# One ones column instead of two, hardware queues only, the last store on the last semaphore, one group's weight sums moved: four small edits to a transformer block bound by TensorE

## The chip, the cores and the metric

The kernel runs on one core of a Trainium2 chip. The metric is the device time of one execution, in microseconds (us); a time below is the median of several executions, with the lowest and highest beside it. A profile shows one execution from inside; its span is about 1.8 us shorter than the device time of the same execution (1271.0 against 1272.77 us for the kernel before), so spans are compared with spans and device times with device times. Engines are named as the profile names them: PE is TensorE's matmul side, PEld its weight load, DVE is VectorE, ACT is ScalarE, POOL is GpSimd, SP is SyncE, which issues most DMAs.

## The reference

A transformer block in bf16: modulation vectors from a small vector `c`, attention of 32 query heads over the last 512 keys of 4 key-value heads, and a gated MLP.

```python
mod = (silu(c) @ w_mod).reshape(1, 6, 1, 1024)        # sa, ca, ga, sb, cb, gb
h = layernorm(x) * (1 + ca) + sa                      # x: 2048 x 1024
q = h @ wq                                            # wq: 1024 x 4096, 32 heads of 128
p = softmax(q k^T * 128**-0.5)                        # k, v: the last 512 of 2048 positions
x = x + ga * ((p v) @ wo)                             # wo: 4096 x 1024
h = layernorm(x) * (1 + cb) + sb
x = x + gb * ((silu(h @ w_gate) * (h @ w_up)) @ w_down)   # 1024 x 3584, 3584 x 1024
```

## The kernel before

The sequence of 2048 rows is worked in four chunks of 512. One chunk and one head make a unit, so there are 128 units. In each unit PE makes scores (`s_ps`), ACT exponentiates them to `pT`, and PE multiplies them with V (`o_ps`): four row tiles times four key tiles, 2048 small matmuls in all. In between, PE makes the queries of a later unit (`q_ps`) and the output projection of an earlier chunk (`a_ps`). After the attention come the MLP's products (`gu_ps`, `d_ps`). The parts that the change touches follow; `[...]` marks cuts.

The divisor of the softmax is made by PE: columns of ones stand beside V, so a column of the product is the row's sum. There are two of them, and only the first is read. Three row tiles share a PSUM bank.

```python
    VN = Dh + 2                                        # Dh = 128
    v_sb = const.tile([P, Hkv, WT, Dh + 32], BF16, name="v_sb")
    [...]
    nc.gpsimd.memset(v_sb[:, :, :, Dh:VN], 1.0)
    [...]
    SLOTS = 3
    def close_bank():
        [...]
        nc.vector.reciprocal(out=rl[:, 0:n], in_=ps[:, 0:n, Dh])
        [...]   # oq = ps[.., 0:Dh] * rl, on DVE
    def emit_o(g):
        [...]
        for t in range(QT):
            if o_slot["n"] == 0:
                o_slot["ps"] = mm("o_ps", (P, SLOTS, VN))
            s_ = o_slot["n"]
            for j in range(WT):
                nc.tensor.matmul(o_slot["ps"][:, s_, :], lhsT=pT[g][:, j, t * P:(t + 1) * P],
                                 rhs=v_sb[:, kv, j, 0:VN], start=(j == 0), stop=(j == WT - 1))
            [...]
            if o_slot["n"] == SLOTS or (t == QT - 1 and h % HQ == HQ - 1):
                close_bank()
```

The first weights for the queries come in pieces of 512 KB; the first of them is loaded in two halves. The loads of V come later, one for each key-value head.

```python
    def load_wq8(i):
        t = blkB("wq8", [P, 2, 8 * P])
        for j in range(2 * i, 2 * i + 2) if i == 0 else ():
            load(t[:, j % 2, :], wq_v[:, j, 0:8 * P])
        if i > 0:
            load(t, wq_v[:, 2 * i:2 * i + 2, 0:8 * P])
    [...]
    def load_v(kv):
        load(v_sb[:, kv, :, 0:Dh], v_v[:, kv])
```

The exponentials are taken without subtracting a maximum. While it runs, the kernel therefore adds up squares of the weights (`bound_wq`, four DVE passes for each group of four heads) and, if a bound is passed, computes everything again by a slower general path behind `tc.If`. With these inputs that path never runs. `at` puts a task into the work of a unit; with `hg` 3 the four passes fall into chunk 1.

```python
    def bound_wq(hg, i, j):
        w = wq_tiles[(1 + hg % (NTC - 1), hg, i)][:, 2 * j:2 * j + 2, :]    # NTC = 4 chunks
        [...]   # one pass of DVE over 128 x 1024, accumulated into sq
    [...]
    at((1 + hg % (NTC - 1)) * H + 4 * hg - LEAD + 2 * i + j, bound_wq, hg, i, j)
    [...]
    def emit_down(cc, dh, t, widths=(512,)):           # the last tile: widths (256, 128, 128)
        [...]
        nc.scalar.dma_start(out=out2d[row:row + P, dsl], in_=o)     # the stores, on ACT's queue
    [...]
        with tc.If(over > 0):
            general_path(tc, *args)                    # three of its DMAs are issued by GpSimd
```

Of the kernel before, what the change touches and what calls it, by code (L numbers as in the profile page):

```python
# [23 lines left out]
def general_path(  # L24
# [16 lines left out]
    nc = tc.nc  # L41
    P = 128
# [3 lines left out]
    H = HD // Dh  # L46
# [121 lines left out]
    with tc.tile_pool(name="atsb", bufs=3) as ap_, tc.tile_pool(  # L168
# [7 lines left out]
        ln_psum["pool"], ln_psum["tag"] = aps, "mm"  # L176
        cT = const.tile([P, DT], BF16, name="cT")
        with nc.allow_non_contiguous_dma(reason="tiny c load"):
            nc.gpsimd.dma_start(out=cT, in_=c_v)
        sig_c = const.tile([P, DT], FP32, name="sig_c")  # L180
        nc.scalar.activation(out=sig_c, in_=cT, func=ACT.Sigmoid)
        siluc = const.tile([P, DT], BF16, name="siluc")
# [12 lines left out]
        with tc.tile_pool(name="p1small", bufs=3) as p1s:  # L195
# [16 lines left out]
            def mod_group(g, late=False):  # L212
                if late:
                    if H * P >= DT * GW:
                        wmf = ap_.tile([P, H, P], BF16, name="wm_l", tag="wo_t", bufs=2)
                        wm = wmf.rearrange("p h q -> p (h q)")[:, 0:DT * GW].rearrange(
                            "p (dt g) -> p dt g", dt=DT)
                    else:
                        wm = ap_.tile([P, DT, GW], BF16, name="wm_l2", tag="wm_late", bufs=2)
                    eng = nc.gpsimd  # L220
                else:
                    wm = op_.tile([P, DT, GW], BF16, name="wm", tag="oT")
                    eng = nc.sync
                with nc.allow_non_contiguous_dma(reason="w_mod column group"):
                    eng.dma_start(out=wm, in_=wm_v[:, :, g * GW:(g + 1) * GW])
                row_ps = aps_s.tile([1, GW], FP32, name="row_ps", tag="s_ps")
                for dt in range(DT):
                    nc.tensor.matmul(row_ps, lhsT=siluc[:, dt:dt + 1], rhs=wm[:, dt, :],
                                     start=(dt == 0), stop=(dt == DT - 1))
                row_sb = ap_.tile([1, GW], FP32, name="row_sb", tag="wq_h", bufs=5)  # L230
                if late:
                    nc.vector.tensor_copy(out=row_sb, in_=row_ps)
                else:
                    nc.scalar.copy(out=row_sb, in_=row_ps)
                for jj in range(JJ):
                    j = (g * GW) // P + jj
                    nc.tensor.matmul(modT_ps[:, j:j + 1], lhsT=row_sb[0:1, jj * P:(jj + 1) * P],
                                     rhs=one11[0:1, 0:1], start=True, stop=True)
                if g == n_first - 1:
                    nc.vector.tensor_copy(out=modT[:, 0:2 * DT], in_=modT_ps[:, 0:2 * DT])  # L240
                    nc.vector.tensor_scalar(out=onepc1, in0=modT[:, DT:2 * DT], scalar1=1.0,
                                            scalar2=None, op0=ALU.add)
                if g == NG - 1:
                    nc.vector.tensor_copy(out=modT[:, 2 * DT:NMOD], in_=modT_ps[:, 2 * DT:NMOD])
                    nc.vector.tensor_scalar(out=onepc2, in0=modT[:, 4 * DT:5 * DT], scalar1=1.0,
                                            scalar2=None, op0=ALU.add)
# [283 lines left out]
    with tc.tile_pool(name="ffw", bufs=2) as fw, tc.tile_pool(  # L530
        name="ffgu", bufs=2) as fgu, tc.tile_pool(
        name="ffsb", bufs=2) as fsb, tc.tile_pool(
        name="ffps", bufs=2, space=bass.MemoryType.PSUM) as fps, tc.tile_pool(
        name="ffps2", bufs=1, space=bass.MemoryType.PSUM) as fps2:
        ln_psum["pool"], ln_psum["tag"] = fps2, "o_ps"
        for f in leftovers:
            f()
        for tci in range(NTC):
            tsl = slice(tci * TCW, (tci + 1) * TCW)
            hsrc = h2T[tci]  # L540
            guT = fgu.tile([P, FT, TCW], BF16, name="guT", tag="guT")
            for fg in range(NFG):
                wg = fw.tile([P, DT, FG * P], BF16, name="wg", tag="wg")
                wu = fw.tile([P, DT, FG * P], BF16, name="wu", tag="wu")
                with nc.allow_non_contiguous_dma(reason="ffn weight slices"):
                    nc.sync.dma_start(out=wg, in_=wg_v[:, :, fg * FG * P:(fg + 1) * FG * P])
                    nc.sync.dma_start(out=wu, in_=wu_v[:, :, fg * FG * P:(fg + 1) * FG * P])
                for fi in range(FG):
                    f = fg * FG + fi
                    g_ps = fps.tile([P, TCW], FP32, name="g_ps", tag="g_ps")  # L550
                    for dt in range(DT):
                        nc.tensor.matmul(g_ps, lhsT=wg[:, dt, fi * P:(fi + 1) * P],
                                         rhs=hsrc[:, dt, :], start=(dt == 0), stop=(dt == DT - 1))
                    u_ps = fps.tile([P, TCW], FP32, name="u_ps", tag="u_ps")
                    for dt in range(DT):
                        nc.tensor.matmul(u_ps, lhsT=wu[:, dt, fi * P:(fi + 1) * P],
                                         rhs=hsrc[:, dt, :], start=(dt == 0), stop=(dt == DT - 1))
                    sig = fsb.tile([P, TCW], BF16, name="sig", tag="sig")
                    nc.scalar.activation(out=sig, in_=g_ps, func=ACT.Sigmoid)
                    g1 = fsb.tile([P, TCW], BF16, name="g1", tag="g1")  # L560
                    nc.vector.tensor_tensor(out=g1, in0=g_ps, in1=sig, op=ALU.mult)
                    nc.vector.tensor_tensor(out=guT[:, f, :], in0=g1, in1=u_ps, op=ALU.mult)
            xf = fsb.tile([P, DT, TCW], BF16, name="xf", tag="xf", bufs=1)
            for dc in range(DT):
                wd = fw.tile([P, FT, P], BF16, name="wd", tag="wd")
                with nc.allow_non_contiguous_dma(reason="w_down column slice"):
                    nc.sync.dma_start(out=wd, in_=wd_v[:, :, dc * P:(dc + 1) * P])
                d_ps = fps.tile([P, TCW], FP32, name="d_ps", tag="d_ps")
                for f in range(FT):
                    nc.tensor.matmul(d_ps, lhsT=wd[:, f, :], rhs=guT[:, f, :],  # L570
                                     start=(f == 0), stop=(f == FT - 1))
                nc.vector.scalar_tensor_tensor(out=xf[:, dc, :], in0=d_ps,
                                               scalar=gb[:, dc:dc + 1], in1=xT[:, dc, tsl],
                                               op0=ALU.mult, op1=ALU.add)
            for qt in range(QT):
                o_ps = fps2.tile([P, DT, P], BF16, name="o_ps", tag="o_ps")
                for dt in range(DT):
                    nc.tensor.transpose(o_ps[:, dt, :], xf[:, dt, qt * P:(qt + 1) * P], ident)
                o_sb = fsb.tile([P, D], BF16, name="o_sb", tag="o_sb")
                if qt % 2 == 0:  # L580
                    nc.vector.tensor_copy(out=o_sb, in_=o_ps.rearrange("p a b -> p (a b)"))
                else:
                    nc.scalar.copy(out=o_sb, in_=o_ps.rearrange("p a b -> p (a b)"))
                row0 = tci * TCW + qt * P
                nc.gpsimd.dma_start(out=out2d[row0:row0 + P, :], in_=o_sb)


@with_exitstack
def fast_path(ctx, tc, flag, A_x, A_k_cache, A_v_cache, A_wq, A_wo, B_x, B_w_gate, B_w_up,
# [119 lines left out]

    def load_wq8(i):  # L710
        t = blkB("wq8", [P, 2, 8 * P])
        for j in range(2 * i, 2 * i + 2) if i == 0 else ():
            load(t[:, j % 2, :], wq_v[:, j, 0:8 * P])
        if i > 0:
            load(t, wq_v[:, 2 * i:2 * i + 2, 0:8 * P])
        wq8.append(t)

    for tt in range(QT):
# [6 lines left out]
    h10 = hpool.tile([P, DT, TCW], BF16, name="hT", tag="hT")  # L725
    load_wm(0, 1)
    kT = blkB("kT", [P, Hkv, W])
    VN = Dh + 2
    v_sb = const.tile([P, Hkv, WT, Dh + 32], BF16, name="v_sb")

    def load_kT(kv):
        pin(nc.sync.dma_start_transpose(
            out=kT[:, kv, :], in_=A_k_cache[0, kv, k0:k0 + W, :]), "dma")

    def load_v(kv):
        load(v_sb[:, kv, :, 0:Dh], v_v[:, kv])

    load_v(0)
    load_wq(0, 2, (0,))
# [2 lines left out]
    for kv in range(1, Hkv):  # L742
        load_kT(kv)
    for kv in range(1, Hkv):
        load_v(kv)

    ones_bf = const.tile([P, P], BF16, name="ones_bf")
    nc.vector.memset(ones_bf, 1.0)
# [88 lines left out]
    def at(k, f, *a):  # L837
        tasks.setdefault(k, []).append((f, a))
# [286 lines left out]
    sq = const.tile([P, NSQ], FP32, name="sq")  # L1125
    gd = const.tile([P, 4], FP32, name="gd")

    def bound_wq(hg, i, j):
        w = wq_tiles[(1 + hg % (NTC - 1), hg, i)][:, 2 * j:2 * j + 2, :]
        junk = wk.tile([P, 2, 512], BF16, name="junk", tag="junk", bufs=1)  # L1130
        col = (hg * 2 + i) * 2 + j
        pin(nc.vector.scalar_tensor_tensor(out=junk, in0=w, scalar=1.0, in1=w, op0=ALU.mult,  # L1132
# [174 lines left out]
    for hg in range(H // 4):  # L1307
        for i in range(2):
            for j in range(2):
                at((1 + hg % (NTC - 1)) * H + 4 * hg - LEAD + 2 * i + j, bound_wq, hg, i, j)  # L1310
    at(NU - H + 2, load_k)
    for kv in range(Hkv):
        at(NU - H + 20 + 2 * kv, bound_k, kv)
# [165 lines left out]
```

## Time and profile before

| | kernel before |
|---|---|
| device time, median of 3 (lowest to highest) | 1272.97 us (1272.22 to 1273.32) |
| span of the profiled execution | 1271.0 us |
| PE busy | 1263.9 us, 99% |
| first `o_ps` matmul starts | 34.03 us |
| first MLP matmul (`gu_ps`) starts | 664.96 us |
| last matmul starts | 1265.92 us |

These are the head of the profile's page, its line of busy times, and the first line of the chain of work that ended last:

```profile
span 1271.0 us, 18169 instructions
PE 1263.9 (99%) x7589; PEld 641.3 (50%) x7589; DVE 608.6 (48%) x1332; ACT 335.6 (26%) x440; POOL 4.2 (0%) x15
PE 97%; DVE 1%; ACT 0%; DMA 0%; POOL 0%; issue 0%; SPq 0%
```

PE is busy nearly always and the chain is almost all PE. Such a kernel is made faster in three ways only: fewer PE columns, fewer gaps of PE, or a shorter head and tail. The 48% of DVE means nothing by itself.

The next view is that of the groups of instructions by shape. Its columns are line, engine, operation, output and inputs, shape, count; then the busy time, the mean duration of one in ns, and the idle time of the engine before them. The second group is the last narrow pieces of the down product.

```profile
L1241 PE MATMUL o_ps<-v_sb,pT 128*128 128x130 bf16 x2048 | 137.0, 220 | 0.1
L1375 PE MATMUL d_ps<-wd,guT 128*128 128x128 bf16 x56 | 3.3, 219 | 0.0
```

The 220 ns are the time of one matmul from its start to its end as the profile models it; matmuls overlap, so what counts is the time from start to start. In the trace that is 56.7 ns for the 130-column `o_ps` matmuls, 55.8 ns for the 128-column `d_ps` pieces and 215.8 ns for 512 columns.

There is one gap of PE in the long middle. The view of windows shows it (columns: start and end in us, then for PE, PEld, DVE, ACT and POOL the busy us and number of instructions, then granted clock, DMA share and GB/s), then come the line of the waits between 200 and 232 us, two lines of PE's timeline and two of DVE's (start us, duration us, engine, line, what):

```profile
215.00:220.00 5.00, 5.00 (x37) 2.77 (x35) 5.00 (x10) 1.94 (x2) 0.00 (x0) 1.00 0.47 115
220.00:225.00 5.00, 5.00 (x24) 2.16 (x22) 5.00 (x13) 2.83 (x5) 0.00 (x0) 1.00 1.01 300
225.00:230.00 5.00, 4.86 (x41) 2.97 (x41) 5.00 (x12) 1.54 (x2) 0.00 (x0) 1.00 0.41 86
545.00:550.00 5.00, 5.00 (x37) 2.76 (x36) 3.63 (x9) 1.72 (x3) 0.00 (x0) 1.00 0.75 239
```

```profile
PEld L1241 <- DVE oq L1228: 0.3, 1, 0.3
```

```profile
223.97 1.03 PE L1209 MATMUL s_ps<-qT,kT 128*128 128x512 bf16 x4
225.14 1.12 PE L1241 MATMUL o_ps<-v_sb,pT 128*128 128x130 bf16 x17
```

```profile
220.80 1.22 DVE L1132 SCALAR_TENSOR_TENSOR junk<-wq 128x1024 bf16<-128x1024 bf16 x1
224.47 0.61 DVE L1228 TENSOR_TENSOR oq<-o_ps,rl 128x128 bf16<-128x128 f32 x2
```

DVE is busy for 15 of 15 us, so it divides an earlier bank of `o_ps` (the `oq` at 224.47 us) late. PE needs that bank back and stands for 0.30 us: four `s_ps` matmuls from 223.97 us would take 0.86 us, but the next one starts only at 225.14. One of the passes over the weights stands in DVE's queue shortly before (220.80 us, 1.22 us).

Three start times cut the execution into pieces: the first `o_ps`, the first `gu_ps` and the last matmul. Here are the first two in the timeline:

```profile
34.03 1.07 PE L1241 MATMUL o_ps<-v_sb,pT 128*128 128x130 bf16 x16
664.96 1.89 PE L1355 MATMUL gu_ps<-hT,wg 128*128 128x512 bf16 x8
```

### The profile page before, as it was taken

How to read it: one execution, taken by the hardware profiler on the slowest of the kernel's cores; microseconds unless marked ns; L12 is line 12 of the kernel's file. 1: busy time of each engine (PE TensorE's matmuls, PEld its weight loads, DVE VectorE, ACT ScalarE, POOL GpSimd, SP SyncE). 2: the span in 40 equal slices, each digit the busy share in tenths (PEclk: the TensorE clock that was granted, in tenths of full speed). 3: DMA queues.
4: the chain of work that ended last, by engine and by line, in shares of the span. 5: the costliest groups of instructions: out<-in, count | busy, mean ns of one | idle time of the engine just before them, and what ended most of it. 6: DMA issues, size and time to landing. Idle time of an engine off the chain costs nothing.

```text
span 1271.0 us, 18169 instructions
## 1 busy us (share of the span) xinstructions
PE 1263.9 (99%) x7589; PEld 641.3 (50%) x7589; DVE 608.6 (48%) x1332; ACT 335.6 (26%) x440; POOL 4.2 (0%) x15
## 2 busy tenths in 40 slices
PE   9999999999999999999999999999999999999998
PEld 4555555555555555555554444444444444444444
DVE  5666658885678664567564631321222112221122
ACT  3543334343333433334341111011100111011100
POOL 1000000000000000000000000000000000000000
PEclk9999999999999999999999999999999999999999
DMA  9997756768456555455585479326633565425702
GB/s 286 211 240 172 186 141 159 182 160 222 122 137 174 150 137 153 113 154 112 121 205 144 130 232 248 95 96 204 220 112 106 169 213 181 158 91 170 244 20 67
DMA packets 306860, 204.46 MB, mean 161 GB/s; under 512 B 145617, under 2 KB 303313, under 8 KB 306770
## 3 DMA queue, kind: packets, MB, share of 16 engines
q1 hardware_dynamic: 301858, 199.03, 57.7%
q10 hardware_dynamic: 4912, 4.20, 1.0%
q8 instruction: 61, 1.00, 0.3%
q14 instruction: 29, 0.24, 0.1%
HBM read 165.94 MB, written 4.21 MB: 134 GB/s over the span
## 4 chain that ended last, share of the span: by engine, by line
PE 97%; DVE 1%; ACT 0%; DMA 0%; POOL 0%; issue 0%; SPq 0%
PE gu_ps L1355 30%; PE a_ps L1273 17%; PE q_ps L1198 16%; PE d_ps L1375 15%; PE o_ps L1241 9%; PE s_ps L1209 8%; PE q_ps L1044 1%; DVE junk L1132 0%; DMA x<-in_A_x_dram 0%; DVE st L847 0%; DVE junk L818 0%; DVE oq L1228 0%; DVE qT L948 0%; DVE f L1286 0%; PE one_ps L1062 0%; DVE f L1285 0%
## 5 line engine op out<-in xcount | busy, mean ns | idle before, releaser
L1211 ACT ACTIVATE pT<-s_ps 128x1024 bf16<-128x1024 f32 x256 | 249.1, 1020 | 345.0 <-PE s_ps L1209 344.9
L1273 PE MATMUL a_ps<-wo,oT 128*128 128x512 bf16 x1024 | 241.9, 379 | 0.0
L1198 PE MATMUL q_ps<-hT,wq 128*128 128x512 bf16 x960 | 227.1, 379 | 0.0
L1361 DVE TENSOR_TENSOR guT<-gu_ps,sg 128x512 bf16<-128x512 f32 x112 | 77.4, 691 | 287.7 <-ACT sg L1360 287.7
L1355 PE MATMUL gu_ps<-hT,wg 128*128 128x512 bf16 x896 | 211.7, 379 | 0.0
L1360 ACT ACTIVATE sg<-gu_ps 128x512 bf16<-128x512 f32 x112 | 66.9, 597 | 488.7 <-PE gu_ps L1355 482.9
L1375 PE MATMUL d_ps<-wd,guT 128*128 128x512 bf16 (+2 forms) x952 | 194.2, 366 | 0.0
L1355 PE MATMUL gu_ps<-hT,wu 128*128 128x512 bf16 x672 | 163.3, 379 | 0.0
L1273 PEld LDWEIGHTS <-oT 128*128 128x128 bf16 x1024 | 100.1, 98 | 120.6
L948 DVE CAST qT<-q_ps 128x512 bf16<-128x512 f32 x121 | 83.6, 691 | 151.9 <-PE q_ps L1198 151.6
L1198 PEld LDWEIGHTS <-wq 128*128 128x128 bf16 x960 | 93.9, 98 | 113.0
L1375 PEld LDWEIGHTS <-guT 128*128 128x128 bf16 x952 | 90.9, 98 | 103.0
L1241 PEld LDWEIGHTS <-pT 128*128 128x128 bf16 x2048 | 126.6, 98 | 30.5 <-issue 0.4
L1355 PEld LDWEIGHTS <-wg 128*128 128x128 bf16 x896 | 87.7, 98 | 105.5
L1241 PE MATMUL o_ps<-v_sb,pT 128*128 128x130 bf16 x2048 | 137.0, 220 | 0.1
L1209 PE MATMUL s_ps<-qT,kT 128*128 128x512 bf16 x512 | 131.5, 379 | 0.0
L1355 PEld LDWEIGHTS <-wu 128*128 128x128 bf16 x672 | 65.7, 98 | 79.3
L1228 DVE TENSOR_TENSOR oq<-o_ps,rl 128x256 bf16<-128x256 f32 (+2 forms) x256 | 100.3, 419 | 3.9
L1379 DVE TENSOR_TENSOR f<-d_ps,gb_bc 128x512 f32<-128x512 f32 (+2 forms) x34 | 22.4, 660 | 140.5 <-PE d_ps L1375 140.5
L1209 PEld LDWEIGHTS <-kT 128*128 128x128 bf16 x512 | 45.0, 98 | 31.2 <-issue 0.5
L1281 DVE TENSOR_TENSOR acc<-a_ps,acc 128x512 f32<-128x512 f32 x64 | 44.0, 687 | 32.6 <-PE a_ps L1273 32.6
L1355 PE MATMUL gu_ps<-hT,v_sb 128*128 128x512 bf16 x224 | 57.5, 379 | 0.0
(101 smaller groups left out, 427.1 us busy)
## 6 DMA issues: line engine op xcount, KB each, us to landing
wo<-in_A_wo_dram SPq DMA_DIRECT2D x64, 512.0 KB
wq<-in_A_wq_dram SPq DMA_DIRECT2D x63, 512.0 KB
wg<-in_B_w_gate_dram SPq DMA_DIRECT2D x56, 512.0 KB
wd<-in_B_w_down_dram SPq DMA_DIRECT2D x56, 512.0 KB
wu<-in_B_w_up_dram SPq DMA_DIRECT2D x42, 512.0 KB
v_sb<-in_B_w_up_dram SPq DMA_DIRECT2D x14, 512.0 KB
x<-in_A_x_dram SPq DMA_DIRECT2D x16, 256.0 KB
wm<-in_w_mod_dram SPq DMA_DIRECT2D x4, 1024.0 KB
```

What stands on the lines that cost most here:

```text
L948: nc.vector.tensor_copy(out=t, in_=q_ps)
L1198: nc.tensor.matmul(q_ps, lhsT=w, rhs=hT[("h1", cc)][:, dt, :], start=(dt == 0), stop=(dt == DT - 1))
L1209: nc.tensor.matmul(s_ps[:, i, :], lhsT=kT[:, kv, j * P:(j + 1) * P], rhs=qT[g], start=True, stop=True)
L1211: nc.scalar.activation(out=p[:, 2 * jj:2 * jj + 2, :], in_=s_ps, func=ACT.Exp, scale=scale)
L1228: nc.vector.tensor_tensor(out=dst, in0=ps[:, s0:s0 + cnt, 0:Dh], in1=sc, op=ALU.mult)
L1241: nc.tensor.matmul(o_slot["ps"][:, s_, :], lhsT=pT[g][:, j, t * P:(t + 1) * P], rhs=v_sb[:, kv, j, 0:VN], start=(j == 0), stop=(j == WT - 1))
L1273: nc.tensor.matmul(a_ps, lhsT=oT[(cc, 2 * q + i)][:, hh % 4, t * P:(t + 1) * P], rhs=wo_tiles[(cc, q, dh, i)][:, hh % 4, :], start=(hh == ...
L1281: nc.vector.tensor_tensor(out=acc[(cc, t)][:, dsl], in0=a_ps, in1=acc[(cc, t)][:, dsl], op=ALU.add)
L1355: nc.tensor.matmul(ps[:, n, :], lhsT=gu_w[(cc, fg, nm, dt // 4)][:, dt % 4, fi * P:(fi + 1) * P], rhs=hT[("h2", cc)][:, dt, :], start=(dt ...
L1360: nc.scalar.activation(out=g, in_=ps[:, 0, :], func=ACT.Silu)
L1361: nc.vector.tensor_tensor(out=guT[(cc, fg)][:, fi, :], in0=ps[:, 1, :], in1=g, op=ALU.mult)
L1375: nc.tensor.matmul(d_ps, lhsT=guT[(cc, f // 4)][:, f % 4, t * P:(t + 1) * P], rhs=wd_tiles[(cc, dh, f // 4)][:, f % 4, c0:c0 + w], start=( ...
```

## The change

Each edit aims at one piece of that time. One ones column less is meant to save one streamed column in 2048 matmuls. The sums of group 3 leave chunk 1, where DVE is full, for the last chunk. The general path uses hardware queues only, and splitting three loads of V (with one load fewer at the start) moves the last store to the last of the eight semaphores that the DMAs take in turn; both are meant to shorten the list of semaphores that SP waits for at the end. The first query-weight piece is loaded whole.

```diff
@@ load_wq8
-        for j in range(2 * i, 2 * i + 2) if i == 0 else ():
-            load(t[:, j % 2, :], wq_v[:, j, 0:8 * P])
-        if i > 0:
-            load(t, wq_v[:, 2 * i:2 * i + 2, 0:8 * P])
+        load(t, wq_v[:, 2 * i:2 * i + 2, 0:8 * P])
@@ V and the ones
-    VN = Dh + 2
+    VN = Dh + 1
-    def load_v(kv):
-        load(v_sb[:, kv, :, 0:Dh], v_v[:, kv])
+    def load_v(kv, j0=0, j1=WT):
+        load(v_sb[:, kv, j0:j1, 0:Dh], v_v[:, kv, j0:j1])
     for kv in range(1, Hkv):
-        load_v(kv)
+        load_v(kv, 0, WT // 2)
+        load_v(kv, WT // 2, WT)
@@ the sums of squares
+    def bound_cc(hg):
+        return NTC - 1 if hg == 3 else 1 + hg % (NTC - 1)
     [...]   # bound_wq and its at(...) use bound_cc(hg) in place of 1 + hg % (NTC - 1)
@@ general_path
-            nc.gpsimd.dma_start(out=cT, in_=c_v)
+            nc.sync.dma_start(out=cT, in_=c_v)
-                    eng = nc.gpsimd
+                    eng = nc.scalar
-                nc.gpsimd.dma_start(out=out2d[row0:row0 + P, :], in_=o_sb)
+                nc.scalar.dma_start(out=out2d[row0:row0 + P, :], in_=o_sb)
```

More of the change, by code (lines that the diff above doesn't have):

```diff
@@ L1126, in fast_path @@
     gd = const.tile([P, 4], FP32, name="gd")
+    def bound_cc(hg):
+        return NTC - 1 if hg == 3 else 1 + hg % (NTC - 1)
     def bound_wq(hg, i, j):
-        w = wq_tiles[(1 + hg % (NTC - 1), hg, i)][:, 2 * j:2 * j + 2, :]
+        w = wq_tiles[(bound_cc(hg), hg, i)][:, 2 * j:2 * j + 2, :]
         junk = wk.tile([P, 2, 512], BF16, name="junk", tag="junk", bufs=1)
@@ L1309, in fast_path @@
             for j in range(2):
-                at((1 + hg % (NTC - 1)) * H + 4 * hg - LEAD + 2 * i + j, bound_wq, hg, i, j)
+                at(bound_cc(hg) * H + 4 * hg - LEAD + 2 * i + j, bound_wq, hg, i, j)
     at(NU - H + 2, load_k)
```

## The prediction

> **What bounds the kernel.** TensorE. The page's busy line has PE busy 99% of a 1271.0 us span; the chain of waits is 97% PE. Between 30 us and the last matmul near 1266 us, the start-to-start times of the matmuls in the trace have only two irregular gaps: 0.20 us at 31.6 us and 0.30 us at 224.6 us. So only fewer PE columns, those gaps, the head (to about 30 us) and the tail (after 1266.1 us) can move the time.
>
> **1. One ones column instead of two.** The 2048 o_ps matmuls stream 129 columns, not 130. In the trace they start 56.7 ns apart; the 128-column pieces of the last down product 55.8 ns apart and the 512-column ones 215.8 ns, so a column costs 0.417 ns. This fits the Trainium skill, page "TensorE: Matmul & The Clock Gate", section "Back-to-back issue gap", N/2.4 + 2.5 ns (56.67 ns for 130). The matmuls are bound by streaming, so all of it is on the chain: 2048 x 0.417 ns = 0.85 us saved. I assume that an odd column count and 516-byte slot steps in PSUM cost nothing.
>
> **2. Weight sums of group 3 moved from chunk 1 to chunk 3.** Four passes of 1.22 us on DVE leave 200 to 222 us, where the windows view shows DVE 5.00 of 5 us busy from 210 to 230 us; there the output division (oq) comes late and PE waits the 0.30 us. They go to about 530 to 550 us, where DVE is busy 2.8 to 3.8 of 5 us. Saves 0.3 us; no new stall.
>
> **3. No software DMA queue in the fallback path.** That path does not run, but the program's end waits for its eight queue semaphores: in the trace's last 2 us SP makes twelve paired waits 0.062 us apart, of which four go. **4. Last store on the last semaphore** (one load fewer at the start, three more for V, so the round robin ends two places on): before, two more waits of 0.066 us follow the one that the last store ends (1269.17 us). Together SP could be ready 0.38 us earlier. But ScalarE, which issues the last store, then branches and reaches the final barrier only at 1269.95 us, 0.23 us before SP (1270.19). So I expect 0.2 to 0.25 us, not 0.38.
>
> **5. Head.** The first query-weight piece now lands whole (before: halves at 10.86 and 11.55 us; PE needs it at 11.48). About 0.1 us of delay is possible, but PE waits for the next piece at 12.95 us anyway. DMA is 99% busy to 27 us, so one issue fewer brings nothing. Splitting the V loads adds three issues of 0.4 to 0.5 us on SP at 29 to 32 us; query weights due at 46.3 and 47.2 us landed at 42.4 and 44.5, so such a delay fits. Net 0, plus or minus 0.2 us.
>
> **Sum.** 0.85 + 0.3 + 0.23 = about 1.4 us, 0.11%: 1272.97 becomes about 1271.6 us. Range 1270.7 to 1272.5. Faster by over 2%: 0.5%; within 2%: 99%; slower by over 2%: 0.5%.
>
> **What would show it.** Right: o_ps matmuls start 56.2 to 56.3 ns apart; no gap near 224 us and none at 530 to 550 us; eight pairs in SP's final waits; ScalarE last into the end barrier; span 1269.5 to 1269.7 us. Wrong: o_ps spacing of 56.7 ns or more; a wait of PE on query weights at 46 us; the gap at 224 us remaining.
>
> **What would make it wrong.** A penalty for 129 columns (1 ns each would cost 2 us); a stall in the head from shifted DMA issue order; between-run noise, which at 1.1 us (1272.22 to 1273.32) is nearly the whole gain.

## The result and the profile after

| | before | after |
|---|---|---|
| device time, median of 6 each (lowest to highest) | 1272.96 us (1272.22 to 1273.32) | 1272.03 us (1271.82 to 1272.32) |
| span of the profiled execution | 1271.0 us | 1270.0 us |

The median became 0.9 us shorter. The ratio of the times is 0.9993, with a 95% interval of 0.998 to 1.0006; a ratio here is the mean time of one kernel's fast runs over that of the other's in the same rounds, so it is not quite the ratio of the medians. The interval includes 1; of the six times of the kernel before, only one (1272.22) lies within the range of the kernel after.

```profile
span 1270.0 us, 18162 instructions
PE 1262.5 (99%) x7589; PEld 641.1 (50%) x7589; DVE 609.4 (48%) x1332; ACT 335.1 (26%) x440; POOL 4.2 (0%) x15
PE 99%; ACT 0%; DMA 0%; POOL 0%; issue 0%; DVE 0%; SPq 0%
```

The group of the small matmuls, by shape:

```profile
L1242 PE MATMUL o_ps<-v_sb,pT 128*128 128x129 bf16 x2048 | 137.0, 220 | 0.0
```

The shape did change from 130 to 129 columns; the busy time of 137.0 us did not change at all. In the trace the start-to-start time is 56.67 ns, as before, and not the 56.2 to 56.3 that was predicted.

The windows and the whole list of waits from 200 to 232 us, and PE's timeline there:

```profile
215.00:220.00 5.00, 5.00 (x37) 2.77 (x35) 4.02 (x8) 1.72 (x3) 0.00 (x0) 1.00 1.16 184
220.00:225.00 5.00, 5.00 (x37) 2.77 (x35) 4.96 (x13) 2.07 (x4) 0.00 (x0) 1.00 0.92 251
225.00:230.00 5.00, 5.00 (x37) 2.77 (x35) 4.11 (x10) 1.94 (x2) 0.00 (x0) 1.00 0.63 124
545.00:550.00 5.00, 5.00 (x36) 2.77 (x35) 4.68 (x10) 1.71 (x3) 0.00 (x0) 1.00 0.62 209
```

```profile
ACT pT L1212 <- PE s_ps L1210: 18.9, 6, 3.3
DVE qT L946 <- PE q_ps L1199: 3.7, 4, 1.0
DVE f L1286 <- PE a_ps L1274: 0.6, 1, 0.6
```

```profile
223.54 1.07 PE L1242 MATMUL o_ps<-v_sb,pT 128*128 128x129 bf16 x16
224.45 1.03 PE L1210 MATMUL s_ps<-qT,kT 128*128 128x512 bf16 x4
```

The wait of PE on `oq` is gone: DVE is busy 13.1 of the 15 us. The passes now fill 545 to 550 us to 4.68 of 5 us, and PE is still busy 5.00 of 5 there. One more thing moved: with DVE free in time, the builder, which orders the instructions itself, put the sixteen `o_ps` before the next unit's `s_ps`; before, they had stood behind them. The new order alone does not explain the missing wait: PE now asks for its bank earlier (223.54 instead of about 224.84 us) and gets it at once.

The first `o_ps` and the first `gu_ps` in the timeline:

```profile
33.60 1.07 PE L1242 MATMUL o_ps<-v_sb,pT 128*128 128x129 bf16 x16
664.20 1.89 PE L1356 MATMUL gu_ps<-hT,wg 128*128 128x512 bf16 x8
```

So the difference of the two spans (1270.99 to 1270.03 us) can be cut at the three start times. All numbers are us:

| piece | before | after | difference | predicted |
|---|---|---|---|---|
| head: to the first `o_ps` | 34.03 | 33.60 | -0.43 | 0, give or take 0.2 |
| attention: first `o_ps` to first `gu_ps` | 630.93 | 630.60 | -0.33 | -0.85 - 0.30 = -1.15 |
| MLP: first `gu_ps` to the last matmul | 600.96 | 600.96 | 0.00 | 0 |
| tail: from the start of the last matmul | 5.07 | 4.86 | -0.21 | -0.2 to -0.25 |

The total of -0.97 lies 0.4 us from the prediction's -1.4, but the parts differ more than the total: the column bought nothing, and the head gave what was not expected of it. Four questions were put to experiments: why the column is free; whether the sums alone account for the 0.3 us; which of the two edits shortens the tail; and whether the head's gain is real.

### The profile page after: what moved, and what is told of

Its sections match the earlier page's. It is cut to its first block, busy times and chain, and to the rows that moved or that the text cites. A ratio compares the mean times of both kernels' runs of the same rounds, so it can differ in the third digit from the quotient of the medians.

```text
span 1270.0 us, 18162 instructions
## 1 busy us (share of the span) xinstructions
PE 1262.5 (99%) x7589; PEld 641.1 (50%) x7589; DVE 609.4 (48%) x1332; ACT 335.1 (26%) x440; POOL 4.2 (0%) x15
## 4 chain that ended last, share of the span: by engine, by line
PE 99%; ACT 0%; DMA 0%; POOL 0%; issue 0%; DVE 0%; SPq 0%
PE gu_ps L1356 30%; PE a_ps L1274 17%; PE q_ps L1199 16%; PE d_ps L1376 15%; PE o_ps L1242 9%; PE s_ps L1210 9%; PE q_ps L1042 1%; DMA x<-in_A_x_dram 0%; PE one_ps L1053 0%; PE mod_ps L785 0%; PE one_ps L1060 0%; PE h_ps L960 0%; ACT junk L981 0%; POOL xn L989 0%; ACT junk L975 0%
## 5 line engine op out<-in xcount | busy, mean ns | idle before, releaser
L1242 PE MATMUL o_ps<-v_sb,pT 128*128 128x129 bf16 x2048 | 137.0, 220 | 0.0
(101 smaller groups left out, 426.7 us busy)
```

## Experiments

Unless said otherwise an edit is made to the kernel after, and a run is one execution with a profile, and correct. "Stretch" is the time from the first `o_ps` to the first `gu_ps`.

### 1. A ladder of widths

Every width from 129 to 136 columns in one kernel, sixteen units of each, with slots spaced by 136 columns so that every slot starts at an even place. One theory says that PE counts columns in pairs. A rival says that an odd spacing of slots in the output costs what the column saves; a third that each column costs its 0.417 ns and something else hid it.

```diff
-    VN = Dh + 1
+    VN = Dh + 8
-                nc.tensor.matmul(o_slot["ps"][:, s_, :], [...]
-                                 rhs=v_sb[:, kv, j, 0:VN], [...]
+                nc.tensor.matmul(o_slot["ps"][:, s_, 0:Dh + 1 + g // 16], [...]
+                                 rhs=v_sb[:, kv, j, 0:Dh + 1 + g // 16], [...]
```

> The changed kernel, but the o_ps matmuls stream 129 columns for units 0 to 15, 130 for 16 to 31, and so on to 136 for units 112 to 127 (256 matmuls of each width; more columns of ones, slots of 136 columns, so every slot starts at an even column; results stay right). Rounding theory (a matmul takes as long as the next even number of columns): start to start 56.67, 56.67, 57.5, 57.5, 58.33, 58.33, 59.17, 59.17 ns. Penalty theory (odd counts or odd slot starts cost a fixed extra, and it happened to be 0.42 ns): the same if the count is to blame, but 56.25 for 129 if the odd slot start was. Floor theory (129 and 130 columns both sit on some floor of 56.67 ns, such as the weight load): 129, 130 equal, then 57.08 for 131 and a step of 0.42 at each width. Linear theory (my prediction): 56.25, 56.67, 57.08 and so on. Span about 2.6 us over the changed kernel under rounding, 3.0 under linear.

The groups by shape between 34 and 670 us (the first five matmuls of 129 columns fall outside that window):

```profile
L1242 PE MATMUL o_ps<-v_sb,pT 128*128 128x135 bf16 x256 | 17.8, 223 | 0.0
L1242 PE MATMUL o_ps<-v_sb,pT 128*128 128x136 bf16 x256 | 17.8, 223 | 0.0
L1242 PE MATMUL o_ps<-v_sb,pT 128*128 128x134 bf16 x256 | 17.6, 222 | 0.0
L1242 PE MATMUL o_ps<-v_sb,pT 128*128 128x133 bf16 x256 | 17.6, 222 | 0.0
L1242 PE MATMUL o_ps<-v_sb,pT 128*128 128x131 bf16 x256 | 17.3, 221 | 0.0
L1242 PE MATMUL o_ps<-v_sb,pT 128*128 128x132 bf16 x256 | 17.3, 221 | 0.0
L1242 PE MATMUL o_ps<-v_sb,pT 128*128 128x130 bf16 x256 | 17.1, 220 | 0.0
L1242 PE MATMUL o_ps<-v_sb,pT 128*128 128x129 bf16 x251 | 16.8, 220 | 0.0
```

The durations go in pairs. The start-to-start times, from the trace, mean of 256 each with a standard error of 0.03 ns:

| columns | 129 | 130 | 131 | 132 | 133 | 134 | 135 | 136 |
|---|---|---|---|---|---|---|---|---|
| ns | 56.67 | 56.67 | 57.50 | 57.50 | 58.32 | 58.38 | 59.17 | 59.16 |

An odd width costs what the next even width costs, with all slots at even places; the odd spacing is not to blame. The stretch says it again: 633.16 us, 2.56 us more than in the kernel after (630.60). With pairs the sum is 512 matmuls each of two, four and six half-steps of 0.417 ns over the cost of 130 columns, 512 x 12 x 0.417 = 2.56 us; with every column counted it would be 256 x (1 + 2 + ... + 7) x 0.417 = 2.99 us. The time was 1274.35 us.

### 2. Two ones columns again, everything else as after

```diff
-    VN = Dh + 1
+    VN = Dh + 2
```

> The changed kernel with two columns of ones again, 130 columns. Rounding theory: o_ps start to start 56.67 ns as with 129, time equal to the changed kernel's (about 1272.0 us; the rest of its gain over the kernel before stays). Linear theory: 0.85 us slower, about 1272.9 us, no gain left over the kernel before but 0.1 us.

Five timed runs: 1272.24 us median (1271.70 to 1272.91), the kernel before beside it 1273.05 (1272.40 to 1273.45, nine runs), ratio 0.9996 with an interval of 0.9982 to 1.001. The group by shape:

```profile
L1242 PE MATMUL o_ps<-v_sb,pT 128*128 128x130 bf16 x2048 | 137.0, 220 | 0.0
```

The stretch is 630.60 us, the same as with one column, and the start-to-start time 56.66 ns. The median lies 0.2 us above that of the kernel after and the profiled execution 0.2 us below it (span 1269.8), so the timed runs decide nothing at this size; the stretch does, to 0.01 us. The column is worth 0.00 us.

### 3. and 4. Odd widths at half clock

Is the unit of counting a pair of columns, or a step of time of 0.83 ns? In the first 4 us PE runs at half speed: the warm-up matmuls of 512 columns start 426.5 ns apart there, not 215.8. A pair of columns takes twice as long then, a step of time stays. The kernel's six warm-up matmuls are replaced by seven of 201 columns and seven of 202.

```diff
-    def warm(n):
+    def warm(n, w=512):
-            nc.tensor.matmul(warm_ps, lhsT=ones_bf, rhs=warm_w, start=True, stop=True)
+            nc.tensor.matmul(warm_ps[:, 0:w], lhsT=ones_bf, rhs=warm_w[:, 0:w], start=True,
+                             stop=True)
-    warm(6)
+    warm(7, 201)
+    warm(7, 202)
```

> The changed kernel with its first six 512-column warm-up matmuls (at 1.6 to 4.2 us, where the trace has them 426 to 427 ns apart, half the later speed) replaced by seven of 201 and seven of 202 columns. If columns are rounded to pairs whatever the array's speed (operand or result handled two columns at a time): both widths start 168.3 ns apart. If the grain is a time of 0.83 ns, which is two columns at the fast speed but one at the slow: 167.5 against 168.3 ns, 6 ns over seven. Nothing else should move; span within 0.5 us of the changed kernel.

The six intervals of each kind had means of 168.5 ns (201 columns) and 168.0 ns (202), with standard errors of 0.7 and 0.6 ns. Worked out from the 426.5 ns of 512 columns, pairs would give 202/512 of it, 168.3, for both; a step of time of 0.83 ns would leave 201 columns their own 201/512, 167.4. The means favour pairs, but not by enough. So the same was run in the other order.

```diff
-    warm(6)
+    warm(7, 202)
+    warm(7, 201)
```

> As cold_odd with the two widths in the other order: seven warm-up matmuls of 202 columns, then seven of 201. cold_odd had 168.5 and 168.0 ns (six intervals each, some 0.5 ns uncertain). Pairs theory: 168.3 for both again. Time-grain theory: 167.5 for 201, 168.3 for 202. Pooled over both runs 0.8 ns should be seen or excluded.

Again 168.7 ns for 201 columns and 168.0 for 202. The twelve intervals of 201 columns together have a mean of 168.58 with a standard error of 0.43 ns, 2.7 standard errors above 167.4. The same came out in either order, so the half-speed runs speak for pairs and against a step of time; the firm evidence remains the ladder at full speed, where the standard error is 0.03 ns. Which side counts in pairs, the operand read from SBUF or the result written to PSUM, no run here tells. The times were 1271.77 and 1271.74 us.

### 5. The sums back in chunk 1

```diff
-        return NTC - 1 if hg == 3 else 1 + hg % (NTC - 1)
+        return 1 + hg % (NTC - 1)
```

> The changed kernel with the weight sums of group 3 back in chunk 1. My theory: the 0.30 us gap of PE before an o_ps matmul comes back near 224 us, and the span grows by 0.3 us. Rival: the gap was an accident of that one run and not of the full DVE; then no gap, the same span.

The wait is back where it was (view of waits, 200 to 232 us, and two lines of PE's timeline):

```profile
PEld L1242 <- DVE oq L1229: 0.3, 1, 0.3
```

```profile
223.71 1.03 PE L1210 MATMUL s_ps<-qT,kT 128*128 128x512 bf16 x4
224.87 1.13 PE L1242 MATMUL o_ps<-v_sb,pT 128*128 128x129 bf16 x17
```

The gap in PE's starts is 0.297 us, the stretch 630.93 us, and the builder's old order (`s_ps`, then `o_ps`) is back too. With the runs so far the two edits that act on the stretch can be set against each other, in us:

| | sums of group 3 in chunk 1 | sums of group 3 in chunk 3 |
|---|---|---|
| 130 columns | 630.93 (before) | 630.60 (two ones) |
| 129 columns | 630.93 (sums in chunk 1) | 630.60 (after) |

The whole gain of the stretch, 0.33 us, is that of the sums, and the column adds nothing in either row. The time was 1272.27 us.

### 6. to 8. The tail: software queue, split loads, both undone

```diff
+# software queue: the three DMAs of general_path on nc.gpsimd again
+# V whole:
-        load_v(kv, 0, WT // 2)
-        load_v(kv, WT // 2, WT)
+        load_v(kv)
```

> The changed kernel with the fallback path's loads and stores on the software queue again: SP's final waits are twelve pairs again. My theory: ScalarE, some 3.14 us after it issued the last store, holds the barrier in any case, so SP is there 3.2 to 3.3 us after that issue (changed kernel: 3.21), at most 0.1 us lost; plus 0.07 us for the longer range of semaphores cleared at the very end (0.81 instead of 0.74 us after the barrier). Rival: the waits add up, four more of 0.062 us, 0.25 us lost, 3.46 us.

> The changed kernel with V in whole loads: the last store is then on the fifth of eight semaphores, no software queue. My theory: ScalarE holds the barrier, so SP is there 3.2 to 3.3 us after the issue of the last store, as in the changed kernel (3.18 to 3.27 in five runs) and sw_queue (3.21). Rival, the three extra waits add up: 3.4 us. Head as in the changed kernel, first o_ps 33.4 to 33.8 us.

> The changed kernel with the software queue in the fallback path and V in whole loads, so the last store is on the fifth of eight semaphores: three more waits of 0.066 us and four more pairs. Now the waits of SP are longer than ScalarE's way: SP 3.35 to 3.55 us after the issue of the last store (the kernel before: 3.36, with two more waits).

The views of the profile leave out semaphore instructions; the trace has them. ACT's branch is the jump over the general path, and "drain" is the instruction with which an engine enters the barrier that ends the program. This is the end of the kernel before and of the kernel after, as the trace's records have it (start in us):

```
before  ACT  1266.831 issues the last store      1267.199 branch   1269.873 next instruction   1269.955 drain
        SP   1269.174 the last store's semaphore (sixth of eight); 1269.240, 1269.308 two more;
             from 1269.373 to 1270.054 twelve waits on two semaphores each; 1270.188 drain
after   ACT  1266.437 branch                     1269.130 next instruction   1269.212 drain
        SP   1268.258 the last store's semaphore (eighth of eight);
             from 1268.324 to 1268.911 eight waits on two each, the last of them held 0.265 us,
             for ACT's semaphore; 1269.283 drain
```

Before, ACT is through first and SP's list is the longer one. After, SP has eight pairs, as predicted, and its last wait is held until ACT is there. Counted from the issue of the last store, in us:

| kernel | queues of the general path | last store on semaphore | ACT drains | SP drains | from there to the end |
|---|---|---|---|---|---|
| before | software | sixth | +3.12 | +3.36 | 0.81 |
| sw_and_v_whole | software | fifth | +3.12 | +3.41 | 0.81 |
| sw_queue | software | eighth | +3.14 | +3.21 | 0.81 |
| v_whole | hardware | fifth | +3.11 | +3.18 | 0.75 |
| after | hardware | eighth | +3.14 | +3.21 | 0.74 |

Either edit alone is enough to make ACT the last, and then SP drains 0.07 us after it. Undoing both brings the list back (+3.41). The second edit of the two buys no more on SP. Without the software queue the time from there to the end is also 0.06 us shorter, because a range of semaphores is cleared in 0.135 us and not 0.178, with the rest in the steps around it; this was so in all fourteen traces. They also bear out the tail as a whole: in the ten in which ACT drains within 0.08 us of SP it takes 4.79 to 4.92 us, in the four with the longer list (before, before_again, sw_and_v_whole and merge_only) 5.07 to 5.27 us. Device times of the three, 1271.90, 1272.27 and 1272.05 us in the order of the texts above, differ by less than their heads do (33.64, 34.09 and 33.60 us to the first `o_ps`) and so say nothing about the tail.

What holds ACT for 2.7 us between its branch and its next instruction? The Trainium skill, page "Runtime: NRT & Kernel Launch", section "Instruction fetch mechanics", says that a taken branch whose target is not in the window already fetched has to fetch the target's page by DMA before going on. The traces fit in part: 2.67 us (before) and 2.69 us (after) pass from the start of the branch to the start of ACT's next instruction, and in the kernel after two 8 KB packets of instruction kind were under way in that time, from 1266.79 to 1267.88 us. A wait for another engine is not the reason: the semaphore that ACT's next instruction asks for was last raised at 1217.54 us, and DVE, which branches 0.68 us before ACT, stands 2.99 us likewise. GpSimd, however, goes on 0.46 us (before) and 0.17 us (after) after its own branch over the general path, at 679.3 us; whether its target had been fetched already is not known. Also, the 1.25 us from the packets' end to ACT's next instruction have no such packet, the trace does not say for which engine a packet was, and no experiment took the branch away, so this is argued and not shown.

### 9. to 12. The head: the first query-weight piece in halves or whole

The first piece was loaded in halves again; to keep the last store on the last semaphore, one load of V was left whole.

```diff
-        load(t, wq_v[:, 2 * i:2 * i + 2, 0:8 * P])
+        for j in range(2 * i, 2 * i + 2) if i == 0 else ():
+            load(t[:, j % 2, :], wq_v[:, j, 0:8 * P])
+        if i > 0:
+            load(t, wq_v[:, 2 * i:2 * i + 2, 0:8 * P])
+        if kv == 1:
+            load_v(kv)
+            continue
```

> The changed kernel with the first query-weight piece loaded in two halves again (V of the second group whole, so that the last store stays on the last semaphore). Theory that one load less is what made the head shorter: the first o_ps matmul starts near 34.0 us as in the kernel before (five runs with the whole piece: 33.42 to 33.77 us), the last of the modulation weights lands near 25.6 us instead of 25.1, span about 1270.4 us. Rival, run-to-run noise of the head: first o_ps within 33.4 to 33.8 us.

The kernel before was profiled a second time, unchanged, to see how far one head lies from another:

> The kernel before, profiled a second time. If its longer head is its own: first o_ps again near 34.0 us. If noise: anywhere in 33.4 to 34.0 us. The 0.30 us gap at 224 us comes again; SP reaches the final barrier 3.3 to 3.5 us after the issue of the last store.

A rival to the halves themselves is the number of loads or their place in the order. So the second piece was halved in place of the first (the same edit with `i == 1`), which leaves the count as in the run before:

> The changed kernel with the second query-weight piece, not the first, in two halves; as many loads as in wq8_halves. If the number of loads early in the queue is what costs: first o_ps at 34.0 to 34.5 us as in wq8_halves (34.50) and the kernel before. If it is the first piece (its small loads just behind the first modulation weights): 33.4 to 33.8 us as in the changed kernel.

And the one load was merged in the kernel before, nothing else:

```diff
-        for j in range(2 * i, 2 * i + 2) if i == 0 else ():
-            load(t[:, j % 2, :], wq_v[:, j, 0:8 * P])
-        if i > 0:
-            load(t, wq_v[:, 2 * i:2 * i + 2, 0:8 * P])
+        load(t, wq_v[:, 2 * i:2 * i + 2, 0:8 * P])
```

> The kernel before with nothing changed but the first query-weight piece loaded whole. If that alone shortens the head: first o_ps at 33.4 to 33.8 us (kernel before: 34.03 and 34.36), about 0.6 us faster than the kernel before, so most of the whole change's gain in one line. The gap at 224 us stays (0.30 us), SP reaches the final barrier 3.35 to 3.55 us after the issue of the last store. Rival, the head needs the other edits too: first o_ps at 34.0 us or later, same time as before.

The first query-weight piece moves between 8 and 11 us. The windows of that time, in the order before, before again, halves, after, merged only, second piece in halves (one fence for each kernel; the last number is GB/s):

```profile
8.00:11.00 3.00, 2.77 (x42) 1.94 (x40) 2.39 (x7) 0.81 (x4) 1.05 (x1) 1.00 0.98 263
```

```profile
8.00:11.00 3.00, 2.42 (x29) 1.45 (x27) 2.64 (x7) 0.99 (x4) 1.20 (x1) 1.00 0.98 275
```

```profile
8.00:11.00 3.00, 2.27 (x27) 1.36 (x26) 1.95 (x4) 0.74 (x4) 1.19 (x1) 1.00 0.99 308
```

```profile
8.00:11.00 3.00, 2.77 (x47) 2.02 (x46) 2.24 (x6) 0.59 (x3) 1.02 (x1) 1.00 1.03 348
```

```profile
8.00:11.00 3.00, 2.77 (x51) 2.11 (x50) 2.25 (x6) 0.59 (x3) 1.03 (x1) 1.00 1.02 353
```

```profile
8.00:11.00 3.00, 2.56 (x36) 1.68 (x34) 1.94 (x5) 0.65 (x3) 1.09 (x1) 1.00 0.99 337
```

The share of DMA time is about 1.0 in all of them: in every kernel the DMA queue was about equally full (the share adds up packets, so it can pass 1 and does not exclude short pauses). The same busy time moves 263 to 308 GB/s where the first piece comes in halves and 337 to 353 where it comes whole. Measured without a fixed window, as the time that the third MiB of all packets in the trace takes (some 50 KB of instructions are among the first), and set against the first `o_ps`, in us:

| kernel | first piece | third MiB takes | first `o_ps` |
|---|---|---|---|
| before | halves | 3.59 | 34.03 |
| before_again | halves | 3.49 | 34.36 |
| wq8_halves | halves | 3.32 | 34.50 |
| second_halves | whole | 3.06 | 33.91 |
| v_whole | whole | 2.81 | 34.09 |
| after | whole | 2.98 | 33.60 |
| merge_only | whole | 2.95 | 33.67 |
| seven other kernels with the piece whole | whole | 2.76 to 3.15 | 33.42 to 33.77 |

The next four MiB take 11.60 to 11.70 us in every one of the fourteen. So halves of the first piece go with a slow third MiB, and one early load more does not by itself (`second_halves` has as many as `wq8_halves`, and its 3.06 us are among those of the whole pieces). The packets that were slow, those of 1 KB and more that took over 150 ns between 8 and 11 us, were 53 to 76 with halves and 1 to 52 without, two ranges that all but touch. Why halves make packets slow, with equal bytes, is not settled by any run.

How much of it reaches the device time is known less well. `v_whole` has a late head although its third MiB was quick, because its second MiB was only through at 8.82 us, against 8.05 to 8.43 in the ten others with the first piece whole; heads vary by some 0.3 us for other reasons. PE's slow start is not one of them: its first warm-up matmul at full speed starts anywhere from 4.6 to 7.8 us in the fourteen traces, and the latest of them (sw_queue) has an early head. Several expectations missed here: before_again (34.36 us) and wq8_halves (34.50) came later than either theory said, second_halves (33.91) fell between the two, and v_whole (34.09) came later than its text said. Five timed runs of merge_only had a median of 1272.61 us (1272.32 to 1272.75) beside 1272.79 (1272.39 to 1273.22) for the kernel before, ratio 0.9998 with an interval of 0.9985 to 1.0012. By their means it is 0.24 us faster, less than the 0.6 expected and within the interval, and its tail was 0.08 to 0.20 us longer than those of the kernel before (5.27 against 5.07 and 5.19 us), because the load that it saves moves the last store to the fifth semaphore. That leaves, as an estimate, 0.3 to 0.4 us for the head, where the traces say 0.6 (mean of the three heads with halves, 34.30, less 33.66, the mean of the eight with the piece whole, both without the kernels with other warm-ups or the second piece in halves). The traces show the direction; the timed runs alone do not, and the size is open between these. Single times: wq8_halves 1272.64, before_again 1273.28, second_halves 1272.07 us.

No version beat both kernels: with two ones columns or with the software queue kept, the kernel is as fast as the one after, within the scatter.

## Why the prediction was right and where not

The class (within 2%), the direction and the range (1270.7 to 1272.5 us) held, and the 1272.03 us measured lie 0.4 us from the 1271.6 predicted. Of its own signs, the gaps, the eight pairs and the last engine came out right; the spacing of the `o_ps` matmuls did not (56.67 ns), and the span of 1270.0 us lay above its 1269.5 to 1269.7. Point by point:

- **What bounds the kernel: right.** The chain is PE in both profiles, and the MLP's 600.96 us did not move by 0.01. Only what was done about columns, gaps, head and tail could count.
- **"2048 x 0.417 ns = 0.85 us saved": wrong; it was 0.00.** The step that failed is the one that followed: "I assume that an odd column count and 516-byte slot steps in PSUM cost nothing." The first half of it is false. 129 columns start 56.67 ns apart, like 130, and 131 like 132 at 57.50; the second half was not the cause, as the ladder had no odd slot step and showed the same. The price of 0.417 ns for a column had been worked out from 128, 130 and 512 columns, all even; it is right as half the price of a pair (57.50 - 56.67 = 0.83 ns) and wrong as the price of one column. The page named in the prediction, section "Back-to-back issue gap", gives N/2.4 + 2.5 ns without that limit: it agrees at 130 (56.67) and fails at 129 (56.25 against 56.67 measured).
- **The sums of group 3: right.** Predicted 0.3 us with no new stall; measured 0.30 us of gap, 0.33 us of stretch, and no gap of PE at 530 to 550 us, though DVE there is fuller than before (4.68 of 5 us). Putting the sums back brings the gap back.
- **The tail: right in mechanism; the size fits in part by luck.** Predicted 0.2 to 0.25 us because ACT would hold SP back; measured 0.21 us in the profiled pair, with eight pairs of waits and ACT last. What the prediction did not see is that either of its two edits would have been enough on SP, and that 0.06 us of the gain is a quicker clearing of semaphores: SP itself drains 0.14 us earlier, not 0.23, because it drains 0.07 us after ACT.
- **"Net 0, plus or minus 0.2 us" for the head: too narrow.** The profiled pair shows 0.43 us, the traces together 0.6, the timed runs 0.3 to 0.4. The reasoning looked at the piece's landing and at PE's next wait and concluded that "one issue fewer brings nothing". The number of issues is indeed not what counts; but with the first piece in halves the packets of that stretch are slower (3.3 to 3.6 us for a MiB and not 2.8 to 3.2), which no count of issues shows. The V loads' three more issues cost PE no wait, as predicted.

A missing 0.85 us and an unforeseen 0.3 to 0.6 us together made a total that looks nearly right; that closeness was luck. Without the experiments the near hit could have been taken for a proof of the column's saving.

## What to carry to other kernels

Before a matmul is trimmed by one column, look whether the count goes from odd to even: here 130 to 129 columns was worth nothing, while 130 to 128 would by estimate be worth a pair (56.67 ns against the 55.8 ns of the 128-column `d_ps` pieces). When several small gains are predicted as a sum, cut the span at a few start times that both kernels share and compare piece with piece, because errors of opposite sign hide in the total. At a program's end, shorten only the list of the engine that reaches the barrier last; once another engine holds it, trimming that list further brings nothing, as with sw_queue and v_whole.

## What the Trainium skill lacked or had wrong

- "TensorE: Matmul & The Clock Gate", section "Back-to-back issue gap": the formula N/2.4 + 2.5 ns held for the even N measured here and not for the odd ones. Odd N cost what N + 1 cost: 129 and 130 columns 56.67 ns, 131 and 132 57.50, 133 and 134 58.32 and 58.38, 135 and 136 59.17 and 59.16.
- The same section calls that formula the gap of an isolated matmul and gives about 81 ns (N = 128) and 131 ns (N = 512) as what a stream of weight loads and matmuls sustains. In this kernel, a stream of such pairs without gaps, it is 55.8 ns at 128 and 215.8 ns at 512 columns; the "isolated" formula (55.8 and 215.8) fits and the sustained figures don't.
- The same page, section "Wait — 56ns, not 53.3ns?": cold matmuls start exactly N/1.2 ns apart. That agrees at 512 columns (426.7, measured 426.5) and at 202 (168.3, measured 168.0), and probably not at 201 (167.5, measured 168.58 with a standard error of 0.43).
- "Runtime: NRT & Kernel Launch", section "Instruction fetch mechanics", names the stall after a taken branch without a figure. Here ScalarE stood 2.6 to 2.7 us between its branch at the program's end and its next instruction, which held SP's last wait in the kernel after; that this is the stall is argued, not shown.
- No page gives the price of the waits that a program makes at its end for the semaphores of its queues: 0.06 to 0.07 us for each wait, on one semaphore or on two, and 0.06 us more at the very end if a software queue is used anywhere, even in a path that does not run.
- "DMA: Bandwidth & Descriptors": its table of bandwidth by size is for DMAs issued from GpSimd and has no row between 64 KB and 1 MB. Nothing there tells why the first 512 KB piece, issued by SP with the DMA queue full, moves slower in two halves (3.3 to 3.6 us for the MiB around it, and not 2.8 to 3.2) when the second piece in halves does not (3.06 us).
